# A two-problem attention decode on one core: softmax weights placed between the V matmuls of the last group, V sums by scaled adds, query projection with half the matmuls

## The chip, the cores and the metric

The kernel runs on one core of a Trainium2 chip. The metric is the device time in microseconds; the kernel before takes 250.23 us as the median of 7 runs (249.08 to 252.08). The engines named below are PE (TensorE, matmuls; PEld is its weight load), DVE (VectorE), ACT (ScalarE), POOL (GpSimd) and SP (SyncE, which here issues nearly all DMAs).

## The reference

Two problems, A and B, with the same shapes: one token `x` (576 wide), 32 query heads over 16 key/value heads, head size 128, 8192 cached positions. A attends to the last W = 2048 positions, B to all 8192. Everything is bf16.

```python
# the same for A (last W positions of the caches) and for B (all of them)
q = (x @ wq).reshape(B, Sq, Hq, Dh).transpose(0, 2, 1, 3)
k = jnp.repeat(k_cache, rep, axis=1)        # rep = 2 query heads to a kv head
v = jnp.repeat(v_cache, rep, axis=1)
scores = jnp.einsum("bhqd,bhkd->bhqk", q, k) * (Dh ** -0.5)
p = softmax(scores, axis=-1)
o = jnp.einsum("bhqk,bhkd->bhqd", p, v)
out = o.transpose(0, 2, 1, 3).reshape(B, Sq, Hq * Dh) @ wo
...
return jnp.concatenate([a, b], axis=-1)
```

## The kernel before

**Data.** About 102.8 MB are read once: `wq` of A and B (4.6 MB each), the K and V caches that are used (five groups of about 16.8 MB) and `wo` of A and B. Group 0 holds all 16 kv heads of A, groups 1 to 4 hold four kv heads of B each (`NG = 5`). A group's K and V lie in four SBUF slots, two for K and two for V; a slot is loaded anew when PE has read it for the last time in the group before. `wq` and `wo` use the same slots ahead of the first and after the last group.

**Stages of a group** (`for g in range(NG)`, L658 to L679). `q_stage` puts the group's query columns into `qst`. `k_transpose` (L460) turns K with PE in eight units; ACT (L472) and DVE (L475) copy the result from PSUM to `kt`. `k_scores` (L480, matmuls L487) adds the scores of all units up in one PSUM bank. `softmax_exp` (L499) takes the maximum, then exp on ACT. `softmax_transpose` (L513) turns the probabilities and DVE writes them, masked, to `ptm` (L527). `v_slot` (L532, matmuls L540) multiplies them with V, 32 matmuls of 512 columns per slot; `opsum` then holds for each row eight blocks of 128 columns, of which the row needs those that belong to its head. `v_keep` (L545) masks all eight blocks into `diag` (L548) and sums them by a reduce (L384, the line of the helper `sums`) into `acc`.

**Query projection** (L411 to L444). The contraction of 576 is cut in nine steps of 64 rows of `wq`; a row's columns are split over a pair of partitions. `x_columns` writes columns of `x`, masked by the parity of the partition, to `xpad`; `q_part` (L417, matmuls L425) runs 9 x 2 x 4 matmuls of 512 columns, into two banks; `q_finish` copies the banks to `qrow` (ACT L431, DVE L433) and turns them with eight small matmuls (L438) into `qcol`. It is done for A, then for B. `wq` of B lies where K slot 1 and the first part of V slot 0 of group 0 go.

**The end.** In the last group, between `softmax_transpose` and `v_slot`, `weights` (L555) works out from the maxima and sums of all rows a factor for each row: three pairs of small fp32 matmuls, `turn` (L558), `back` (L576), `total` (L588), with short DVE and ACT steps between them. `combine(0)` (L602) scales A's `acc` (L599) and adds A's partial rows up per head with fp32 matmuls (L612), also ahead of the last group's V. After the loop `combine(1)` does that for groups 1 to 4. Then `wo_part` (L622, matmuls L627) runs 128 matmuls of 144 columns for A and 128 for B, `finish_out` (L632) copies each result (L633) and SP sends it (L639). `wo` of A is one load, `wo` of B four (L681 to L690): 24 rows into K slot 1, then 5, 2 and 1 rows into V slot 0 and behind, the first of these three after the last group's reads of V slot 0.

**Order of work.** `add` (L53) records operations in program order; each engine runs its own in that order, and waits come from what each operation reads and writes. DVE, ACT, POOL and SP are unrolled. PE runs its part of the groups as a loop of five passes (L231) with one body: an operation's `loop=(g, place, cond)` gives its place in the body, and neighbouring places with the condition `LAST` (the last group only) are put together in an `If` (L227), a branch on PE.

Of the kernel before, what the change touches and what calls it, by code (L numbers as in the profile page):

```python
# [275 lines left out]
def bass_concat_heads__sliding_block_cached__gqa_block_cached__decode_kernel(  # L276
# [37 lines left out]
    sameB = nc.alloc_sbuf_tensor("sameB", [128, 128], F32)  # L314
    selq = nc.alloc_sbuf_tensor("selq", [128, 4], BF16)
    onesf = nc.alloc_sbuf_tensor("onesf", [128, 4], F32)
    qst = nc.alloc_sbuf_tensor("qst", [128, 2 * 264], BF16)
    qcol = nc.alloc_sbuf_tensor("qcol", [128, 2, HQ], BF16)
    xtwo = nc.alloc_sbuf_tensor("xtwo", [128, 2, 8], BF16)
    xpad = nc.alloc_sbuf_tensor("xpad", [128, 2, 10, 32], BF16)  # L320
    par2 = nc.alloc_sbuf_tensor("par2", [128, 2], F32)
    maskV = nc.alloc_sbuf_tensor("maskV", [128, 8], F32)
    qrow = nc.alloc_sbuf_tensor("qrow", [128, 1024], BF16)
    stat = nc.alloc_sbuf_tensor("stat", [128, 40], F32)
    srow = nc.alloc_sbuf_tensor("srow", [4, 2, 160], F32)
    diag = nc.alloc_sbuf_tensor("diag", [128, 8, DH], F32)
    acc = nc.alloc_sbuf_tensor("acc", [128, NG, DH], F32)
# [43 lines left out]
    def select(t, base_, pattern, mult):  # L371
        return lambda pool: pool.affine_select(out=t, in_=t, compare_op=ALU.not_equal, fill=1.0,
                                               base=base_, pattern=pattern, channel_multiplier=mult)

    add("pool", select(ident[:], 0, [[-1, 128]], 1), reads=["ident"], writes=["ident"])
    add("pool", select(selq[:], 0, [[-32, 4]], 1), reads=["selq"], writes=["selq"])
    for dj in range(-3, 4):
# [31 lines left out]


    def x_columns(P):  # L411
        for e in range(2):
            add("dve", lambda dve, e=e: dve.tensor_scalar(xpad[:, P, 5 * e:5 * e + 5, 0], xtwo[:, P, 0:5],  # L413
                                                          par2[:, e:e + 1], None, ALU.mult),
                reads=[("xtwo", P), "par2"], writes=[("xpad", P)])

    def q_part(P, off, res):  # L417
        def mm(pe):
            for u in range(9):
                for c in range(2):  # L420
                    for j in range(4):
                        n_ = 2 * j + c
                        x = u // 2 if n_ // 4 == u % 2 else 5 + (u + 1) // 2
                        o = off + u * 2048 + (n_ % 4) * 512
                        ins = pe.matmul(opsum[32 * j:32 * j + 32, c * 512:(c + 1) * 512], lhsT=xpad[:, P, x, :],  # L425
                                        rhs=slots[:, o:o + 512], start=(u == 0), stop=(u == 8))
            return ins
        add("pe", mm, reads=[("xpad", P)] + res, writes=B_O)

    def q_finish(P):  # L430
        add("act", lambda act: act.activation(qrow[:, 0:512], opsum[:, 0:512], ACT.Copy),  # L431
            reads=[B_O[0]], writes=[("qrow", 0)])
        add("dve", lambda dve: dve.tensor_copy(qrow[:, 512:1024], opsum[:, 512:1024]),  # L433
            reads=[B_O[1]], writes=[("qrow", 1)])

        def tr(pe):
            for i in range(8):
                ins = pe.matmul(misc[:, i * 4:(i + 1) * 4], lhsT=qrow[:, i * 128:(i + 1) * 128],  # L438
                                rhs=selq[:, :], start=True, stop=True)
            return ins  # L440
        add("pe", tr, reads=[("qrow", 0), ("qrow", 1), "selq"], writes=[B_M])
        add("dve", lambda dve: dve.tensor_copy(qcol[:, P, :].rearrange("p (j i) -> p i j", j=4),
                                               misc[:, 0:32].rearrange("p (i j) -> p i j", j=4)),
            reads=[B_M], writes=[("qcol", P)])  # L444
# [51 lines left out]
    def st(col, n=1):  # L496
        return stat[:, col:col + n]
# [33 lines left out]

    def v_slot(g, s, place):  # L532
        v = slots[:, voff(s):voff(s) + SLOT].rearrange("p (m y) -> p m y", m=4)

        def mm(pe):
            for tt in range(8):
                for j in range(4):
                    o = tt * 128 + 32 * j
                    b = (8 * j + tt) * 128
                    ins = pe.matmul(opsum[32 * j:32 * j + 32, s * 512:(s + 1) * 512], lhsT=ptm[:, o:o + 32],  # L540
                                    rhs=v[:, :, b:b + 128], start=(tt == 0), stop=(tt == 7), skip_group_check=True)
            return ins
        add("pe", mm, reads=["ptm"] + VS[s], writes=[B_O[s]], loop=(g, place, None))

    def v_keep(g):  # L545
        def go(dve):
            m = bass.AP(tensor=maskV, offset=0, ap=[[8, 128], [1, 8], [0, DH]])
            return dve.tensor_tensor(diag[:, :, :], opsum[:, :].rearrange("p (y d) -> p y d", y=8), m, ALU.mult)  # L548
        add("dve", go, reads=B_O + ["maskV"], writes=["diag"], tag="keep")
        sums(acc[:, g, :], diag[:, :, :].rearrange("p y d -> p d y"), ["diag"], [("acc", g)])  # L550


    LAST = lambda g: g == NG - 1

    def weights(g):  # L555
        at = [(g, 18.1 + k / 8, LAST) for k in range(3)]

        def turn(pe):  # L558
            pe.matmul(misc[0:1, 0:128], lhsT=st(C_M), rhs=identf[:, :], start=True, stop=True)  # L559
            return pe.matmul(misc[0:4, 128:256], lhsT=st(C_M + 1, 4), rhs=identf[:, :], start=True, stop=True)  # L560
        add("pe", turn, reads=[("st", C_M + c) for c in range(NG)] + ["identf"], writes=[B_M], loop=at[0])

# [11 lines left out]
        add("dve", rep, reads=["srow"], writes=["srow2"])  # L574

        def back(pe):  # L576
            pe.matmul(misc[:, 256:257], lhsT=srow[0:1, 0, 32:160], rhs=onesf[0:1, 0:1], start=True, stop=True)  # L577
            return pe.matmul(misc[:, 257:261], lhsT=srow[0:4, 1, 32:160], rhs=identf[0:4, 0:4], start=True, stop=True)  # L578
        add("pe", back, reads=["srow2", "ones", "identf"], writes=[B_M], loop=at[1])
        add("dve", lambda dve: dve.scalar_tensor_tensor(st(C_T, NG), st(C_M, NG), SCALE, misc[:, 256:261],  # L580
# [5 lines left out]
            reads=[("st", C_W)] + [("st", C_L + c) for c in range(NG)], writes=[("st", C_T + 5)])  # L586

        def total(pe):  # L588
            pe.matmul(misc[:, 264:265], lhsT=same[:, :], rhs=st(C_T + 5), start=True, stop=True)  # L589
            return pe.matmul(misc[:, 265:269], lhsT=sameB[:, :], rhs=st(C_T + 6, 4), start=True, stop=True)  # L590
        add("pe", total, reads=[("st", C_T + 5), "same", "sameB"], writes=[B_M], loop=at[2])
        add("dve", lambda dve: dve.reciprocal(st(C_T + 10, NG), misc[:, 264:269]),
# [4 lines left out]

    def scaled(g):
        add("dve", lambda dve: dve.tensor_scalar(accs[:, g, :], acc[:, g, :], st(C_AL + g), None, ALU.mult),  # L599
            reads=[("acc", g), ("st", C_AL)], writes=[("accs", g)])  # L600

    def combine(P, loop=None):  # L602
        groups = range(1, NG) if P else [0]
        for g in groups:
            scaled(g)

        def mm(pe):
            for g in groups:
                for r in range(4):
                    w = pickB[:, r, :] if P else pick[:, r, :]  # L610
                    to = misc[32 * (g - 1):32 * g, 0:32] if P else misc[:, 0:32]
                    ins = pe.matmul(to, lhsT=w, rhs=accs[:, g, 32 * r:32 * r + 32], start=(r == 0), stop=(r == 3))  # L612
            return ins
        add("pe", mm, reads=["pickB" if P else "pick"] + [("accs", g) for g in groups], writes=[B_M], loop=loop)
        add("dve", lambda dve: dve.tensor_copy(opj[:, P, 0:32], misc[:, 0:32]), reads=[B_M], writes=[("opj", P)])

# [41 lines left out]
    for g in range(NG):  # L658
        for s in range(2):
            load_kv(ks, g, s, koff(s), KS[s], "k")  # L660
        for s in range(2):
            load_kv(vs, g, s, voff(s), VS[s], "v")
        for s in range(2):
            q_stage(g, s)
        k_transpose(g, 0, 0)
        k_transpose(g, 1, 1)
        for u in range(2, 8):
            k_scores(g, u - 2, 2 * u)
            k_transpose(g, u, 2 * u + 1)
        k_scores(g, 6, 16)  # L670
        k_scores(g, 7, 17)
        softmax_exp(g)
        softmax_transpose(g, 18)
        if g == NG - 1:
            weights(g)
            combine(0, (g, 18.6, LAST))
        v_slot(g, 0, 20)
        v_slot(g, 1, 21)
        v_keep(g)  # L679

# [6 lines left out]
    for k, (P, lo, n, off, res) in enumerate(wo_loads):  # L687
        if res[0][0] == "w":
            wo_loads[k] = (P, lo, n, off, res)
        load_wo(P, lo, n, off, res)  # L690
    combine(1)
    for P in range(2):
# [35 lines left out]
```

## Time and profile before

The profile is one execution with the hardware profiler. "Busy" is the time in which an engine worked; the line numbers are those of the listing.

| what | value |
|---|---|
| time of 7 runs | median 250.23 us, 249.08 to 252.08 |
| profiled execution, device time | 251.18 us |
| its span, first to last instruction | 249.7 us |
| mean granted TensorE clock | 0.835 of full |
| DMA, mean rate over the span | 412 GB/s, 102.89 MB |
| PE / PEld busy | 165.2 us / 117.3 us |
| DVE / ACT busy | 87.3 us / 87.3 us |
| q matmuls L425 | x144, 11.5 us |
| V matmuls L540 | x320, 28.4 us |
| mask L548 and reduce L384 of the V sums | x5 each, 1225 ns and 1871 ns |
| combine L612 | x8 with `pick` 1.9 us, x32 with `pickB` 1.4 us |
| projection matmuls L627 | x256, 6.4 us |

A group is read as: line, engine, operation, how many, busy time or mean of one. An fp32 matmul appears as two records, so the 4 and 16 matmuls of the two combines stand as x8 and x32. Matmuls overlap their weight loads, so the busy times of PE and PEld are not added.

### The profile page before, as it was taken

What the parts mean: (1) busy time and instruction counts of PE and PEld (TensorE: products, weight loads), DVE (VectorE), ACT (ScalarE), POOL (GpSimd) and SP (SyncE); (2) the same over time, 40 slices, a digit from 0 to 9 for tenths busy, and PEclk for the clock granted to TensorE, in tenths of its full rate; (3) what the DMA queues carried; (4) which work ended last, traced back from release to release, by engine and by line L of the source; (5) the groups of instructions that cost most, each with busy time, mean ns of one, the idle gap of its engine ahead of it and who ended that gap; (6) DMA issues with size and microseconds to landing.
All of it is one profiled execution on the core that took longest, in us unless ns stands there. A gap on an engine that the chain in (4) does not pass through costs nothing. (4 is left out here: it accounts for less than half of the span.)

```text
span 249.7 us, 5439 instructions
## 1 busy us (share of the span) xinstructions
PE 165.2 (66%) x2428; PEld 117.3 (47%) x2428; DVE 87.3 (35%) x140; ACT 87.3 (35%) x95; POOL 10.7 (4%) x48
## 2 busy tenths in 40 slices
PE   0027739993725999463999471999570899558474
PEld 0003329781315876223886221987330878345163
DVE  0001034553141555231656222456314355431500
ACT  2000017873002786101778100677500578500000
POOL 7400000000000000000000000000000000000000
PEclk9999797999595999775999775699978699955759
DMA  9998999999999999999999999999999999999970
GB/s 337 419 431 373 424 392 417 424 424 419 450 430 436 430 446 432 420 430 430 426 430 446 436 425 430 430 425 430 446 425 436 425 436 425 430 437 433 428 307 7
DMA packets 5929, 102.89 MB, mean 412 GB/s; under 512 B 928, under 2 KB 1056, under 8 KB 1312
## 3 DMA queue, kind: packets, MB, share of 16 engines
q1 hardware_dynamic: 5632, 102.77, 96.8%
q8 instruction: 6, 0.10, 0.2%
q10 hardware_dynamic: 288, 0.00, 0.1%
q14 instruction: 3, 0.02, 0.0%
HBM read 102.76 MB, written 0.00 MB: 412 GB/s over the span
## 5 line engine op out<-in xcount | busy, mean ns | idle before, releaser
L472 ACT ACTIVATE kt<-ktps 128x1024 bf16<-128x1024 bf16 x80 | 78.4, 1021 | 89.1 <-PE ktps L466 89.1
L466 PE MATMUL ktps<-ident,slots 128*128 128x128 bf16 x1280 | 87.5, 233 | 33.2 <-PEq L214 30.9
L466 PEld LDWEIGHTS ktps<-ident,slots 128*128 128x128 bf16 x1280 | 81.3, 105 | 48.7 <-issue 48.5
L475 DVE COPY kt<-ktps 128x1024 bf16<-128x1024 bf16 x80 | 55.3, 692 | 69.5 <-PE ktps L466 69.5
L540 PE MATMUL opsum<-slots,ptm 128*32 128x512 bf16 x320 | 28.4, 533 | 4.2 <-PEq L214 4.2
L487 PE MATMUL sacc<-kt,qst 128*32 128x512 bf16 x320 | 25.4, 393 | 1.8 <-PEq L214 1.8
L425 PE MATMUL opsum<-slots,xpad 128*32 128x512 bf16 x144 | 11.5, 490 | 19.8 <-DVE xpad L413 19.8
L540 PEld LDWEIGHTS opsum<-slots,ptm 128*32 128x32 bf16 x320 | 11.6, 128 | 19.6 <-issue 17.2
L425 PEld LDWEIGHTS opsum<-slots,xpad 128*32 128x32 bf16 x144 | 5.1, 119 | 25.2 <-issue 23.6
L548 DVE TENSOR_TENSOR diag<-opsum,maskV 128x1024 f32<-128x1024 f32 x5 | 6.1, 1225 | 29.0 <-PE opsum L540 29.0
L518 PE MATMUL misc<-ident,psb 128*128 128x128 bf16 x40 | 4.1, 264 | 11.5 <-PEq L214 11.5
L431 ACT ACTIVATE qrow<-opsum 128x512 bf16<-128x512 f32 x2 | 1.2, 597 | 28.3 <-PE opsum L425 28.3
L456 POOL COPY qst<-qcol 128x8 bf16<-128x8 bf16 x20 | 3.1, 191 | 165.5 <-PE sacc L487 150.6
L508 ACT ACTIVATE psb<-sacc,stat 128x1024 bf16<-128x1024 f32 x5 | 5.6, 1113 | 11.8 <-DVE stat L502 11.8
L518 PEld LDWEIGHTS misc<-ident,psb 128*128 128x128 bf16 x40 | 3.1, 117 | 14.0 <-issue 14.0
L384 DVE TENSOR_REDUCE acc<-diag 128x128 f32<-128x1024 f32 x5 | 9.4, 1871 | 0.2
L487 PEld LDWEIGHTS sacc<-kt,qst 128*32 128x32 bf16 x320 | 5.0, 94 | 7.9 <-issue 4.2
L527 DVE TENSOR_SCALAR ptm<-misc,par 128x512 bf16<-128x512 bf16 x10 | 4.4, 480 | 11.2 <-PE misc L518 11.2
L627 PE MATMUL ktps<-slots,opj 128*32 128x144 bf16 x256 | 6.4, 268 | 2.7 <-issue 2.7
L627 PEld LDWEIGHTS ktps<-slots,opj 128*32 128x32 bf16 x256 | 5.7, 118 | 3.2 <-issue 3.2
L413 DVE TENSOR_SCALAR xpad<-xtwo,par 128x5 bf16<-128x5 bf16 x4 | 0.7, 232 | 14.5 <-DMA xtwo<-in_A_x_dram 13.0
L433 DVE CAST qrow<-opsum 128x512 bf16<-128x512 f32 x2 | 1.4, 692 | 11.8 <-PE opsum L425 11.8
(60 smaller groups left out, 35.3 us busy)
## 6 DMA issues: line engine op xcount, KB each, us to landing
slots<-in_B_k_cache_dram SPq DMA_DIRECT2D x8, 4096.0 KB
slots<-in_B_v_cache_dram SPq DMA_DIRECT2D x8, 4096.0 KB
slots<-in_A_k_cache_dram SPq DMA_DIRECT2D x8, 1024.0 KB
slots<-in_A_v_cache_dram SPq DMA_DIRECT2D x8, 1024.0 KB
slots<-in_A_wq_dram SPq DMA_DIRECT2D x1, 4608.0 KB, 13.9
slots<-in_B_wq_dram SPq DMA_DIRECT2D x1, 4608.0 KB, 24.7
slots<-in_A_wo_dram SPq DMA_DIRECT2D x1, 4608.0 KB, 19.5
slots<-in_B_wo_dram SPq DMA_DIRECT2D x1, 3456.0 KB, 27.4
```

What stands on the lines that cost most here:

```text
L384: add("dve", lambda dve: dve.tensor_reduce(out, view, AX.X, ALU.add), reads=reads, writes=writes, tag=tag)
L425: ins = pe.matmul(opsum[32 * j:32 * j + 32, c * 512:(c + 1) * 512], lhsT=xpad[:, P, x, :], rhs=slots[:, o:o + 512], start=(u == 0), stop=( ...
L466: ins = pe.matmul(ktps_bf[q][:, t * 128:(t + 1) * 128], lhsT=slots[:, o:o + 128], rhs=ident[:, :], start=True, stop=True, is_transpose=True)
L472: add("act", lambda act, q=q, dst=dst: act.activation(dst, ktps_bf[q], ACT.Copy), reads=[("bank", q)], writes=[("kt", u % NKT, q)], tag="e ...
L475: add("dve", lambda dve, q=q, dst=dst: dve.tensor_copy(dst, ktps_bf[q]), reads=[("bank", q)], writes=[("kt", u % NKT, q)], tag="e%d%d" % ( ...
L487: ins = pe.matmul(sacc[32 * j:32 * j + 32, :], lhsT=qst[:, o:o + 32], rhs=rhs, start=(u == 0 and e == 0), stop=True, skip_group_check=True)
L508: return act.activation(psb[:, :].rearrange("p (x g) -> p x g", g=2), src, ACT.Exp, bias=st(C_NB + g), scale=SCALE, accum_out=st(C_L + g))
L518: ins = pe.matmul(dst[:, t * 128:(t + 1) * 128], lhsT=psb[:, t * 128:(t + 1) * 128], rhs=ident[:, :], start=True, stop=True, is_transpose= ...
L527: ins = dve.tensor_scalar(to, src, par2[:, e:e + 1], None, ALU.mult)
L540: ins = pe.matmul(opsum[32 * j:32 * j + 32, s * 512:(s + 1) * 512], lhsT=ptm[:, o:o + 32], rhs=v[:, :, b:b + 128], start=(tt == 0), stop=( ...
L548: return dve.tensor_tensor(diag[:, :, :], opsum[:, :].rearrange("p (y d) -> p y d", y=8), m, ALU.mult)
L627: ins = pe.matmul(ktps[P][32 * j:32 * j + 32, 0:OUTW], lhsT=opj[:, P, jj:jj + 32], rhs=slots[:, o:o + OUTW], start=(jj == 0), stop=(jj == ...
```

## The change

The query projection now uses 36 matmuls for each problem: `xpad` carries two columns per step, one for each half of the output columns, and `q_part` writes both halves at once into one bank; `q_finish` has one copy and four turning matmuls. `v_keep` is called once for each slot and adds four blocks with a factor from a mask column, directly from PSUM; in the last group the factor is `wlast`, the mask times the last group's softmax factor, and the sum goes straight to `accs`. `v_slot` is cut in halves of 16 matmuls. `weights` is cut in three parts, which stand in the last group ahead of the first V half, between the halves of slot 0, and after slot 0. `combine` of groups 0 to 3 stands between the halves of slot 1, ahead of the last V matmuls; after the loop only group 4 is combined. A's result column copy (`o_columns(0)`) stands before the last half. PE's conditional pieces in the loop body are now four instead of one.

```diff
-    selq = nc.alloc_sbuf_tensor("selq", [128, 4], BF16)
+    selq = nc.alloc_sbuf_tensor("selq", [128, 4, 2], BF16)
-    xpad = nc.alloc_sbuf_tensor("xpad", [128, 2, 10, 32], BF16)
+    xpad = nc.alloc_sbuf_tensor("xpad", [128, 2, 9, 32], BF16)
-    qrow = nc.alloc_sbuf_tensor("qrow", [128, 1024], BF16)
+    qrow = nc.alloc_sbuf_tensor("qrow", [128, 512], BF16)
-    diag = nc.alloc_sbuf_tensor("diag", [128, 8, DH], F32)
+    wlast = nc.alloc_sbuf_tensor("wlast", [128, 8], F32)
...
-    add("pool", select(selq[:], 0, [[-32, 4]], 1), reads=["selq"], writes=["selq"])
+    add("pool", select(selq[:], 0, [[-32, 4], [-1, 2]], 1), reads=["selq"], writes=["selq"])
...
     def x_columns(P):
-        for e in range(2):
-            add("dve", lambda dve, e=e: dve.tensor_scalar(xpad[:, P, 5 * e:5 * e + 5, 0], xtwo[:, P, 0:5],
-                                                          par2[:, e:e + 1], None, ALU.mult),
+        for u, n, col, i, e in ((0, 5, 0, 0, 0), (0, 5, 1, 0, 1), (1, 4, 0, 1, 1), (1, 4, 1, 0, 0)):
+            dst = bass.AP(tensor=xpad, offset=(P * 9 + u) * 32 + col, ap=[[576, 128], [64, n]])
+            add("dve", lambda dve, dst=dst, i=i, n=n, e=e: dve.tensor_scalar(dst, xtwo[:, P, i:i + n], par2[:, e:e + 1],
+                                                                             None, ALU.mult),
                 reads=[("xtwo", P), "par2"], writes=[("xpad", P)])
     def q_part(P, off, res):
         def mm(pe):
             for u in range(9):
-                for c in range(2):
-                    for j in range(4):
-                        n_ = 2 * j + c
-                        x = u // 2 if n_ // 4 == u % 2 else 5 + (u + 1) // 2
-                        o = off + u * 2048 + (n_ % 4) * 512
-                        ins = pe.matmul(opsum[32 * j:32 * j + 32, c * 512:(c + 1) * 512], lhsT=xpad[:, P, x, :],
-                                        rhs=slots[:, o:o + 512], start=(u == 0), stop=(u == 8))
-            return ins
-        add("pe", mm, reads=[("xpad", P)] + res, writes=B_O)
+                for j in range(4):
+                    o = off + u * 2048 + j * 512
+                    ins = pe.matmul(opsum[32 * j:32 * j + 32, P * 512:(P + 1) * 512], lhsT=xpad[:, P, u, :],
+                                    rhs=slots[:, o:o + 512], start=(u == 0), stop=(u == 8))
+            return ins
+        add("pe", mm, reads=[("xpad", P)] + res, writes=[B_O[P]])
     def q_finish(P):
-        add("act", lambda act: act.activation(qrow[:, 0:512], opsum[:, 0:512], ACT.Copy),
-            reads=[B_O[0]], writes=[("qrow", 0)])
-        add("dve", lambda dve: dve.tensor_copy(qrow[:, 512:1024], opsum[:, 512:1024]),
-            reads=[B_O[1]], writes=[("qrow", 1)])
+        add("act", lambda act: act.activation(qrow[:, :], opsum[:, P * 512:(P + 1) * 512], ACT.Copy),
+            reads=[B_O[P]], writes=["qrow"])
         def tr(pe):
-            for i in range(8):
-                ins = pe.matmul(misc[:, i * 4:(i + 1) * 4], lhsT=qrow[:, i * 128:(i + 1) * 128],
-                                rhs=selq[:, :], start=True, stop=True)
-            return ins
-        add("pe", tr, reads=[("qrow", 0), ("qrow", 1), "selq"], writes=[B_M])
-        add("dve", lambda dve: dve.tensor_copy(qcol[:, P, :].rearrange("p (j i) -> p i j", j=4),
-                                               misc[:, 0:32].rearrange("p (i j) -> p i j", j=4)),
+            for i in range(4):
+                ins = pe.matmul(misc[:, i * 8:(i + 1) * 8], lhsT=qrow[:, i * 128:(i + 1) * 128],
+                                rhs=selq[:, :, :].rearrange("p j h -> p (j h)"), start=True, stop=True)
+            return ins
+        add("pe", tr, reads=["qrow", "selq"], writes=[B_M])
+        add("dve", lambda dve: dve.tensor_copy(qcol[:, P, :].rearrange("p (h j i) -> p i j h", h=2, j=4),
+                                               misc[:, 0:32].rearrange("p (i j h) -> p i j h", i=4, j=4)),
             reads=[B_M], writes=[("qcol", P)])
...
         add("dve", put, reads=[B_M, "par2"], writes=["ptm"], tag="put")
-    def v_slot(g, s, place):
+    def v_slot(g, s, half, place):
         v = slots[:, voff(s):voff(s) + SLOT].rearrange("p (m y) -> p m y", m=4)
         def mm(pe):
-            for tt in range(8):
+            for tt in range(4 * half, 4 * half + 4):
                 for j in range(4):
                     o = tt * 128 + 32 * j
                     b = (8 * j + tt) * 128
...
             return ins
         add("pe", mm, reads=["ptm"] + VS[s], writes=[B_O[s]], loop=(g, place, None))
-    def v_keep(g):
-        def go(dve):
-            m = bass.AP(tensor=maskV, offset=0, ap=[[8, 128], [1, 8], [0, DH]])
-            return dve.tensor_tensor(diag[:, :, :], opsum[:, :].rearrange("p (y d) -> p y d", y=8), m, ALU.mult)
-        add("dve", go, reads=B_O + ["maskV"], writes=["diag"], tag="keep")
-        sums(acc[:, g, :], diag[:, :, :].rearrange("p y d -> p d y"), ["diag"], [("acc", g)])
+    def v_keep(g, s):
+        last = g == NG - 1
+        dst = accs[:, g, :] if last else acc[:, g, :]
+        res = ("accs" if last else "acc", g)
+        for m in range(4):
+            w = (wlast if last else maskV)[:, 4 * s + m:4 * s + m + 1]
+            src = opsum[:, s * 512 + m * 128:s * 512 + (m + 1) * 128]
+            if s == 0 and m == 0:
+                add("dve", lambda dve, w=w, src=src: dve.tensor_scalar(dst, src, w, None, ALU.mult),
+                    reads=[B_O[s], "wlast" if last else "maskV"], writes=[res], tag="keep")
+            else:
+                add("dve", lambda dve, w=w, src=src: dve.scalar_tensor_tensor(dst, src, w, dst, ALU.mult, ALU.add),
+                    reads=[B_O[s], "wlast" if last else "maskV", res], writes=[res], tag="keep")
     LAST = lambda g: g == NG - 1
-    def weights(g):
-        at = [(g, 18.1 + k / 8, LAST) for k in range(3)]
-
+    def weights_top(g):
         def turn(pe):
             pe.matmul(misc[0:1, 0:128], lhsT=st(C_M), rhs=identf[:, :], start=True, stop=True)
             return pe.matmul(misc[0:4, 128:256], lhsT=st(C_M + 1, 4), rhs=identf[:, :], start=True, stop=True)
-        add("pe", turn, reads=[("st", C_M + c) for c in range(NG)] + ["identf"], writes=[B_M], loop=at[0])
+        add("pe", turn, reads=[("st", C_M + c) for c in range(NG)] + ["identf"], writes=[B_M], loop=(g, 18.5, LAST))
         def top(dve):
             dve.tensor_reduce(srow[0:1, 0, 0:32], misc[0:1, 0:128].rearrange("p (j h) -> p h j", j=4), AX.X, ALU.max)
...
             return dve.tensor_scalar(srow[0:4, 1, 32:160].rearrange("p (a r) -> p a r", r=8), src, -SCALE, None, ALU.mult)
         add("dve", rep, reads=["srow"], writes=["srow2"])
+    def weights_exp(g):
         def back(pe):
             pe.matmul(misc[:, 256:257], lhsT=srow[0:1, 0, 32:160], rhs=onesf[0:1, 0:1], start=True, stop=True)
             return pe.matmul(misc[:, 257:261], lhsT=srow[0:4, 1, 32:160], rhs=identf[0:4, 0:4], start=True, stop=True)
-        add("pe", back, reads=["srow2", "ones", "identf"], writes=[B_M], loop=at[1])
+        add("pe", back, reads=["srow2", "ones", "identf"], writes=[B_M], loop=(g, 20.1, LAST))
         add("dve", lambda dve: dve.scalar_tensor_tensor(st(C_T, NG), st(C_M, NG), SCALE, misc[:, 256:261],
                                                         ALU.mult, ALU.add),
             reads=[B_M] + [("st", C_M + c) for c in range(NG)], writes=[("st", C_T)])
...
         add("dve", lambda dve: dve.tensor_tensor(st(C_T + 5, NG), st(C_W, NG), st(C_L, NG), ALU.mult),
             reads=[("st", C_W)] + [("st", C_L + c) for c in range(NG)], writes=[("st", C_T + 5)])
+    def weights_sum(g):
         def total(pe):
             pe.matmul(misc[:, 264:265], lhsT=same[:, :], rhs=st(C_T + 5), start=True, stop=True)
             return pe.matmul(misc[:, 265:269], lhsT=sameB[:, :], rhs=st(C_T + 6, 4), start=True, stop=True)
-        add("pe", total, reads=[("st", C_T + 5), "same", "sameB"], writes=[B_M], loop=at[2])
+        add("pe", total, reads=[("st", C_T + 5), "same", "sameB"], writes=[B_M], loop=(g, 20.3, LAST))
         add("dve", lambda dve: dve.reciprocal(st(C_T + 10, NG), misc[:, 264:269]),
             reads=[B_M], writes=[("st", C_T + 10)])
         add("dve", lambda dve: dve.scalar_tensor_tensor(st(C_AL, NG), st(C_W, NG), 2.0, st(C_T + 10, NG),
                                                         ALU.mult, ALU.mult),
             reads=[("st", C_T + 10), ("st", C_W)], writes=[("st", C_AL)])
-    def scaled(g):
-        add("dve", lambda dve: dve.tensor_scalar(accs[:, g, :], acc[:, g, :], st(C_AL + g), None, ALU.mult),
-            reads=[("acc", g), ("st", C_AL)], writes=[("accs", g)])
-
-    def combine(P, loop=None):
-        groups = range(1, NG) if P else [0]
-        for g in groups:
-            scaled(g)
-
+        add("dve", lambda dve: dve.tensor_scalar(wlast[:, :], maskV[:, :], st(C_AL + NG - 1), None, ALU.mult),
+            reads=["maskV", ("st", C_AL)], writes=["wlast"])
+        for k in range(NG - 1):
+            add("dve", lambda dve, k=k: dve.tensor_scalar(accs[:, k, :], acc[:, k, :], st(C_AL + k), None, ALU.mult),
+                reads=[("acc", k), ("st", C_AL)], writes=[("accs", k)])
+    def combine(groups, loop=None):
         def mm(pe):
             for g in groups:
                 for r in range(4):
-                    w = pickB[:, r, :] if P else pick[:, r, :]
-                    to = misc[32 * (g - 1):32 * g, 0:32] if P else misc[:, 0:32]
+                    w = pickB[:, r, :] if g else pick[:, r, :]
+                    to = misc[32 * (g - 1):32 * g, 304:336] if g else misc[:, 272:304]
                     ins = pe.matmul(to, lhsT=w, rhs=accs[:, g, 32 * r:32 * r + 32], start=(r == 0), stop=(r == 3))
             return ins
-        add("pe", mm, reads=["pickB" if P else "pick"] + [("accs", g) for g in groups], writes=[B_M], loop=loop)
-        add("dve", lambda dve: dve.tensor_copy(opj[:, P, 0:32], misc[:, 0:32]), reads=[B_M], writes=[("opj", P)])
+        add("pe", mm, reads=["pick", "pickB"] + [("accs", g) for g in groups], writes=[B_M], loop=loop)
+    def o_columns(P):
+        add("dve", lambda dve: dve.tensor_copy(opj[:, P, 0:32], misc[:, 272 + 32 * P:304 + 32 * P]),
+            reads=[B_M], writes=[("opj", P)])
     def load_wo(P, lo, n, off, res):
...
         softmax_exp(g)
         softmax_transpose(g, 18)
         if g == NG - 1:
-            weights(g)
-            combine(0, (g, 18.6, LAST))
-        v_slot(g, 0, 20)
-        v_slot(g, 1, 21)
-        v_keep(g)
+            weights_top(g)
+        v_slot(g, 0, 0, 20)
+        if g == NG - 1:
+            weights_exp(g)
+        v_slot(g, 0, 1, 20.2)
+        if g == NG - 1:
+            weights_sum(g)
+        v_keep(g, 0)
+        v_slot(g, 1, 0, 21)
+        if g == NG - 1:
+            combine(range(NG - 1), (g, 21.2, LAST))
+            o_columns(0)
+        v_slot(g, 1, 1, 21.5)
+        v_keep(g, 1)
     wo_loads = [
         (0, 0, 32, 0, [("k", 0), ("k", 1, 0)]),
...
         load_wo(P, lo, n, off, res)
-    combine(1)
+    combine([NG - 1])
+    o_columns(1)
     for P in range(2):
         for Q, lo, n, off, res in wo_loads:
             if Q == P:
```

## Prediction, made before the changed kernel ran

> **What bounds the kernel now.** I read the page's slices first, then transfers by line, then the chain of waits from its end backward.
>
> ```profile
> PEclk9999797999595999775999775699978699955759
> DMA  9998999999999999999999999999999999999970
> q8 instruction: 6, 0.10, 0.2%
> slots<-in_B_wo_dram SPq DMA_DIRECT2D x1, 3456.0 KB, 27.4
> slots<-in_B_wo_dram SPq DMA_DIRECT2D x1, 720.0 KB, 12.8
> slots<-in_B_wo_dram SPq DMA_DIRECT2D x1, 288.0 KB, 13.1
> slots<-in_B_wo_dram SPq DMA_DIRECT2D x1, 144.0 KB, 13.0
> ```
>
> Each digit of the DMA row covers 6.24 us: the 16 DMA engines are full from 1.3 us to about 241. Nothing that makes an engine faster before 241 shortens the run, unless the DMA queue had run dry there, and it doesn't (in-flight packets average 15.3 of 16 at worst, around 35 us). The last number of the B_wo lines is the time from issue to landing. With the issue times of the timeline (215.06, then 231.37, 231.74, 232.21) they land at 242.4, 244.1, 244.8 and 245.2. So what can be won lies in the last 8 us:
>
> ```profile
> 227.79 5.89 PE opsum L540 x63
> 233.68 0.02 issue
> 233.70 1.24 DVE diag L548
> 234.94 0.02 issue
> 234.96 1.87 DVE acc L384
> 236.83 0.79 DVE accs L599 x4
> 237.62 0.04 issue
> 237.67 1.20 PE misc L612 x29
> 238.87 3.40 PE ktps L627 x92
> 242.27 1.35 issue
> 243.62 2.18 PE ktps L627 x127
> 245.80 1.38 issue
> 247.18 0.55 PE ktps L627 x21
> 247.73 0.02 issue
> 247.75 0.31 DVE outsb L633
> ```
>
> Columns: start, length, what. The last V (L540), sums (L548, L384), scaling (L599), head combine (L612), output projections of A and then B (L627). The landings bind nothing here: B's matmuls begin at about 244.2 (20 of the 127 still belong to A, whose result is copied at 244.17), 1.8 us after 242.4, and its last 21 come at 247.18, 2 us after 245.2. The two "issue" gaps, 2.73 us together, are PE waiting for its own code: of the six 16 KB packets of q8, four fall before 67 us and two at 241.3 and 244.8, just ahead of the gaps; 127 matmuls with as many weight loads between the gaps are 254 instructions, one block (an estimate: 256 of 64 bytes).
>
> From PE's last matmul to the span's end it is 2.0 us (249.73 - 247.73: copy 0.31, issue and landing of a 1 KB output).
>
> **The change, part by part.**
>
> *q from half the matmuls.* L425 falls from 72 to 36 matmuls per problem and L438 from 8 to 4; two tiny xpad writes are added (L413 rows: 0.23 us each). At 5.76 us for 72, q of B ends 2.9 us earlier, less 0.3. This lies under the DMA row; k loads of group 0 issue earlier and fill a dip of under 0.1 us. Worth 0 to -0.1 us. DVE's qrow copy goes (0.69), ACT's stays; hidden too. Its real effect is on code: 72+72+8+8 = 160 PE instructions fewer ahead of the loop.
>
> *V sums.* Per group, L548 1.22 + L384 1.87 = 3.1 us become eight scaled adds of 128x128 from PSUM. No row shows such an add. The nearest is L599, the same size from SBUF: 0.28 each, 0.20 stepping back to back. An eighth of L548 (0.15) is the lower bound; with every add waiting for its predecessor I bound it above by 0.4. I take 0.25: four after the last V matmul make 1.0 us (0.6 to 1.6). Groups 0 to 3: PE waits 6.1 to 7.3 us for K there anyway; 0.
>
> *Weights between V matmuls.* New PE order from ptm ready (220.39): turn 1.03 (L559+L560) to 221.4; V half 1.48 (a quarter of 5.93) to 222.9, over DVE's 0.9 us for L564 to L573; back 1.02 to 223.9; V half to 225.4, over stat and exp (0.17+0.21+0.18 and handovers); total 1.02 to 226.4; V half to 227.9. DVE from 226.4: reciprocal, weight, wlast, four accs: 0.20+0.18+0.15+0.80 and handovers, 227.9 to 228.1. Combine of groups 0 to 3: 1.91 (pick) + 24/32 of 1.20 = 2.8 to 230.9. Last half to 232.4, adds 1.0 to 233.4, combine of group 4 0.3 + handovers: A's projection starts at **233.8 instead of 238.8**. Three more branches round the conditional pieces: the one in a non-last group takes 0.37 us on PE's sequencer, so up to 1.1 us per group, inside the 6 us wait; in the last group the end moves to 234.9 at worst.
>
> *What is late next.* A's projection: 128 matmuls at 33.7 ns (108 in 238.63 to 242.27) = 4.3, so 238.1. B's then waits for its 3456 KB at 242.4, 4.3 us later. Hence all of V, sums and combine has 4.3 us of cover, and their errors above cost nothing. The three small B_wo loads wait for V slot 0: issued at 225.4 instead of 231.4. SP has nothing else queued behind them but the outputs, yet the engines have A_wo and B_wo ahead of them until 241, so they land as before (0; bounds -0.5 to +0.5).
>
> B's 128 matmuls from 242.4 then set the end, and their price is the clock. Rows: 33.7 ns at granted 0.5, 17.2 ns (127 in 2.18) at 1.0.
>
> ```profile
> 232.40:235.80 3.40, 1.25 (x24) 0.41 (x16) 2.06 (x2) 0.00 (x0) 0.00 (x0) 1.00 1.00 431
> 235.80:239.20 3.40, 1.53 (x51) 1.53 (x55) 1.95 (x6) 0.00 (x0) 0.00 (x0) 0.50 0.90 384
> 242.60:246.00 3.40, 2.18 (x127) 2.00 (x128) 0.31 (x1) 0.00 (x0) 0.00 (x0) 0.99 0.12 42
> ```
>
> Stretches with PE busy first and the granted clock third from the end: after a stretch with PE busy 1.25 of 3.4 us, the next ran at 0.5; B ran at 0.99 because A kept PE busy just before. The rule that speaks against the change is in the Trainium skill, "TensorE: Matmul & The Clock Gate", What's actually happening: an idle window of about 3.4 us puts the clock at half, and a busy one is needed to get it back. The new 4.3 us hole before B is such an idle window. By the clock of the old B the matmuls take 2.2 us, but the last landing (245.2 + 4 matmuls) gives 245.35, end 247.35, **-2.4**. By the rule they take 4.3 us: 242.43 + 4.31 = 246.75, end 248.75, **-1.0**. The 1.25-of-3.4 row is nearest to the new hole, so I take -1.0.
>
> *Code.* 160 instructions less, a few more for branches and waits: boundaries move later in the projections by some 77 matmuls. The one after A's 108th comes at B's 57th, the next at 235+77 = 312, beyond 256: one late block vanishes. The one before, one block further back (old: in the combine after the loop), comes at A's 57th; in the old run the code behind it was there in time, having been fetched in the loop's first pass. The block for B's 57th can be asked for from A's 57th on, at 235.7, and is needed at 244.3. In the old kernel 243.62 to 247.18, 3.6 us, passed between entering one block and having the next; under full DMA, by the packets, 5 to 10. I take it as there in time: 0, bound +1.5 (asked for only at 242.4: there at 246.0, 71 matmuls at 33.7 ns to 248.4, end 250.4).
>
> **Sum** against the profiled run's own 249.73: 248.75, -0.98. That run was 251.18 in all (1.45 outside the span), 0.95 above the median; I take its excess for something both kernels have, so 250.23 - 1.0 = **249.2**.
>
> **Rivals.**
>
> 1. *Landings alone set the end.* B runs at the full clock, or the lagging engine that brings the last B_wo rows is earlier: 247.85 from the sum above, down to 247. For it: windows are not aligned to the program, and busy shares of 64% (2.18 of 3.4) kept the clock. Against it: 4.3 us of nothing.
>
> 2. *The code wait stays on the path*, as bounded: end 250.4, +0.7, 250.9. For it: four fetches under full DMA were slow, and one stalled PE in the first pass. Against it: over 8 us of notice.
>
> 3. *Slower: the loop no longer stays in PE's instruction memory.* Old boundaries count back from the 108th matmul in steps of one block: the loop lay in four blocks, its start a little (some 135 instructions) behind a boundary. With 160 fewer ahead of it the start falls before that boundary: five blocks, six with the one prefetched.
>
> ```profile
> 58.89 0.38 PE L466 MATMUL ktps<-ident,slots 128*128 128x128 bf16 x4 [2.23 <-issue]
> ```
>
> That is a block arriving late in the first pass (timeline; the bracket is the wait): 2.23 us. The Trainium skill, "Runtime: NRT & Kernel Launch", Instruction fetch mechanics, gives PE 128 KiB (eight blocks of 16 KiB) but also says that only a two-page window is kept and a taken branch out of it costs a fetch. By the two-page rule the old loop would have refetched on every pass; between 70 and 240 us there is no q8 packet, so at least five blocks stayed. If five are all, every pass fetches all: 5 x 2.23 = 11.2 us less 6.9 of slack = 4.3, times 4 passes = +17, about 267. It decides from the sixth block on. Eight blocks by the page against five proved: unlikely.
>
> 4. *The change doesn't shorten the chain* (V, combine and weights stall each other by more than 4.3 us): 250 to 252. The sum has no wait of that size.
>
> **How the numbers follow.** Forecast 50%, rival 1 20%, rival 2 14%, rival 3 7%, rival 4 and others 9%. The forecast's own range is 248.2 to 250.2 (landing ±0.5, run-to-run ±0.5). A measurement tells some 0.5% from no change, 248.98 to 251.48. Faster: all of rival 1 and about half of the forecast, 0.45. Same: the other half, rival 2, some of rival 4: 0.38. Slower: rival 3 and the rest, 0.17. The range 247.2 to 251.0 leaves out the loop's reload and the extremes.
>
> **What would show it.** A's projection starts near 234 and B's after a hole that ends at 242.4 by a DMA, not by "issue"; granted clock 0.5 over B; B's length 4.3 us; one L627 issue gap or none; q8 packets five or six, none between 75 and 230 us. Wrong if: q8 packets recur in every pass (rival 3); B at 17 ns (rival 1); A starts after 238 (rival 4); the B_wo landings move by over 1 us.

## The result, and the profile after

The changed kernel takes **248.47 us** (median of 14 runs, 247.9 to 249.5) against 250.23 (35 runs of the kernel before): ratio 0.9932, 95% interval 0.9915 to 0.9950. That is 1.8 us less. The forecast was 249.2 with a range of 247.2 to 251.0.

The profiled execution has a span of 246.9 us. Its chain of waits from 236 us on (start, length, what), its transfers by line (last number: us from issue to landing), and, ahead of them, its row of q8, the queue whose 16 KB packets the prediction reads as PE's code:

```profile
213.55 27.69 DMA slots<-in_B_wo_dram
241.24 0.04 issue
241.28 3.59 PE ktps L634 x128
244.88 0.02 issue
244.90 0.31 DVE outsb L640
```

```profile
q8 instruction: 6, 0.10, 0.2%
...
slots<-in_B_wo_dram SPq DMA_DIRECT2D x1, 3456.0 KB, 27.7
slots<-in_B_wo_dram SPq DMA_DIRECT2D x1, 720.0 KB, 18.4
slots<-in_B_wo_dram SPq DMA_DIRECT2D x1, 288.0 KB, 18.8
slots<-in_B_wo_dram SPq DMA_DIRECT2D x1, 144.0 KB, 18.6
```

Where the old chain went back through V, mask, reduce and combine and had two "issue" waits of 1.35 and 1.38 us inside the projections, the new one has a transfer: B's 24 rows of `wo`, landed at 241.24. B's 128 matmuls follow in one piece, then the copy. The three small loads are issued at 224.5 to 225.4 instead of 231.4 to 232.2 and take 5.6 us more from issue to landing: they land 1.2 us earlier, as the 24 rows do, so the earlier issue itself brought nothing that can be seen. PE's work ahead of B and in B, over the last windows (the columns are PE busy with its count, then PEld, DVE, ACT, POOL, granted clock, DMA share, GB/s):

```profile
237.40:240.80 3.40, 0.37 (x18) 0.18 (x6) 0.31 (x1) 0.00 (x0) 0.00 (x0) 1.00 0.86 351
240.80:244.20 3.40, 2.92 (x100) 2.92 (x104) 0.00 (x0) 0.00 (x0) 0.00 (x0) 0.50 0.42 161
244.20:246.90 2.70, 0.64 (x40) 0.45 (x28) 0.31 (x1) 0.00 (x0) 0.00 (x0) 1.00 0.00 0
```

PE worked 0.37 of 3.4 us ahead of B, and B ran at half the clock until 244.2, when it came back.

### The profile page after: what moved, and what is told of

It is laid out like the page before. It is cut to its first block, busy times and chain, and to the rows that moved or that the text cites. A ratio compares the mean times of both kernels' runs of the same rounds, so it can differ in the third digit from the quotient of the medians.

```text
span 246.9 us, 5330 instructions
## 1 busy us (share of the span) xinstructions
PE 166.6 (67%) x2348; PEld 117.9 (48%) x2348; DVE 84.8 (34%) x172; ACT 87.2 (35%) x95; POOL 10.7 (4%) x48
## 5 line engine op out<-in xcount | busy, mean ns | idle before, releaser
L538 PE MATMUL opsum<-slots,ptm 128*32 128x512 bf16 x320 | 33.1, 579 | 5.8 <-PEq L214 5.8
L538 PEld LDWEIGHTS opsum<-slots,ptm 128*32 128x32 bf16 x320 | 12.8, 132 | 21.0 <-issue 19.4
L425 PE MATMUL opsum<-slots,xpad 128*32 128x512 bf16 x72 | 8.1, 629 | 21.7 <-DVE xpad L416 21.7
L425 PEld LDWEIGHTS opsum<-slots,xpad 128*32 128x32 bf16 x72 | 2.9, 140 | 25.1 <-issue 25.1
L555 DVE SCALAR_TENSOR_TENSOR acc<-opsum,maskV,acc 128x128 f32<-128x128 f32 x28 | 9.8, 351 | 7.3 <-PE opsum L538 6.4
L634 PE MATMUL ktps<-slots,opj 128*32 128x144 bf16 x256 | 7.6, 310 | 3.5 <-DMA slots<-in_B_wo_dram 3.5
L634 PEld LDWEIGHTS ktps<-slots,opj 128*32 128x32 bf16 x256 | 7.2, 141 | 3.7 <-DMA slots<-in_B_wo_dram 3.7
L416 DVE TENSOR_SCALAR xpad<-xtwo,par 128x5 bf16<-128x5 bf16 (+1 forms) x8 | 1.3, 232 | 16.0 <-DMA xtwo<-in_A_x_dram 12.9
L552 DVE TENSOR_SCALAR acc<-opsum,maskV 128x128 f32<-128x128 f32 x4 | 1.4, 351 | 15.0 <-PE opsum L538 15.0
L498 DVE TENSOR_REDUCE stat<-sacc 128x1 f32<-128x512 f32 x5 | 3.5, 692 | 4.4 <-PE sacc L485 4.4
```

The lines of the kernel that those rows point to most:

```text
L425: ins = pe.matmul(opsum[32 * j:32 * j + 32, P * 512:(P + 1) * 512], lhsT=xpad[:, P, u, :], rhs=slots[:, o:o + 512], start=(u == 0), stop=( ...
L498: add("dve", lambda dve: dve.tensor_reduce(st(C_M + g), sacc[:, :], AX.X, ALU.max), reads=[B_S], writes=[("st", C_M + g)], tag="max")
L555: add("dve", lambda dve, w=w, src=src: dve.scalar_tensor_tensor(dst, src, w, dst, ALU.mult, ALU.add), reads=[B_O[s], "wlast" if last else ...
L634: ins = pe.matmul(ktps[P][32 * j:32 * j + 32, 0:OUTW], lhsT=opj[:, P, jj:jj + 32], rhs=slots[:, o:o + OUTW], start=(jj == 0), stop=(jj == ...
```

## The experiments

The theory after the result: the end was a PE chain with two late code blocks in it, and is now "B's rows landed + 128 matmuls + 2.0 us". Whatever takes some 2 us off the PE chain should reach this new limit, so the parts of the change should not add up. The rivals: the V chain (weights, sums) makes the gain; or the code position makes it; or the lag of one DMA engine in the old profile is a property of the kernels.

Each median is of 6 to 12 runs. They came from two chips, at three times; the ratio is always to the kernel before, run beside them.

| kernel | median us | before beside it | ratio, 95% interval |
|---|---|---|---|
| q_alone | 248.26 | 250.3 | 0.9928, 0.9904 to 0.9951 |
| v_alone | 248.50 | 250.3 | 0.9945, 0.9914 to 0.9977 |
| code_only | 248.41 | 250.3 | 0.9928, 0.9903 to 0.9954 |
| split_wo | 248.03 | 250.3 | 0.9918, 0.9885 to 0.9950 |
| weights_front | 248.71 | 249.75 | 0.9958, 0.9939 to 0.9977 |
| sums_old | 248.28 | 249.75 | 0.9940, 0.9919 to 0.9962 |
| both_old | 247.94 | 249.75 | 0.9926, 0.9898 to 0.9954 |
| code_full | 249.85 | 250.2 | 0.9998, 0.9969 to 1.0027 |
| warm8 | 247.90 | 250.2 | 0.9899, 0.9869 to 0.9930 |
| split_warm | 247.80 | 250.2 | 0.9893, 0.9862 to 0.9924 |
| after_again | 248.68 | 250.2 | 0.9936, 0.9902 to 0.9969 |

### The kernel before, a second profile

> The kernel before once more, for a second profile. If the DMA engine that landed B's rows 1.5 us after the other fifteen belonged to that one execution, the lag is under 0.5 us here and the 24 rows land at about 241; the two waits for code in the projections stay, 1.3 to 1.4 us each. If the lag belongs to the kernel, it is 1.5 us again.

No edit; one execution, 249.27 us, span 247.8. Its chain of waits at the end:

```profile
237.10 3.40 PE ktps L627 x105
240.50 1.22 issue
241.72 2.18 PE ktps L627 x127
243.90 1.38 issue
245.28 0.55 PE ktps L627 x21
245.83 0.02 issue
245.85 0.31 DVE outsb L633
```

The two waits are there again, at the same matmuls. The 24 rows landed at 240.45 by the semaphore updates of the 16 DMA engines, the slowest of them 0.10 us after the fifteenth; in the first profile it was 1.53 us (242.41 against 240.88). In none of the ten other profiles that load the 24 rows at once is it over 0.5 us. So the lag belonged to that execution, while the two code waits came in both.

### The query projection alone, and V alone

```diff
# q_alone: the kernel before with the new selq, xpad, qrow, x_columns, q_part, q_finish
-                        ins = pe.matmul(opsum[32 * j:32 * j + 32, c * 512:(c + 1) * 512], lhsT=xpad[:, P, x, :],
+                    ins = pe.matmul(opsum[32 * j:32 * j + 32, P * 512:(P + 1) * 512], lhsT=xpad[:, P, u, :],
...
# v_alone: the changed kernel with the old selq, xpad, qrow, x_columns, q_part, q_finish
```

> The kernel before with only the new query projection (160 PE instructions fewer ahead of the loop). Code-position theory: no wait for code in A's projection, at most one short one near B's 57th matmul, A still starts at about 238.8; the tail loses 1.4 us and up to 2.4 where the landings allow it: 248.9 us (248.0 to 249.4). Rival, the V chain (sums and weights) made the whole gain: 250.2, within 0.3 of the kernel before.

> The changed kernel with the old query projection (code longer by 160 instructions again). Cover theory: A's projection starts at about 234, a wait for code near A's 105th matmul disappears in the hole before B's data, none is seen in B: 248.5 to 249.0, like the full change. Rival, the code position made the gain: 250.2.

Each half gives what the whole gives: 0.9928 and 0.9945 against 0.9932. q_alone's chain, with the V part as it was:

```profile
214.31 26.53 DMA slots<-in_B_wo_dram
240.84 0.04 issue
240.88 1.12 PE ktps L623 x60
242.00 1.14 issue
243.15 1.28 PE ktps L623 x68
```

A ran without a code wait; B waited for its data until 240.84 and then for code after its 60th matmul (expected at the 57th). So q_alone does not end where the changed kernel does for the same reason. From the landing of the 24 rows to B's last matmul it took 3.58 us, at the full clock but with 1.14 us of waiting for code; the changed kernel took 3.63 us, with no such wait but mostly at the half clock. The two prices happen to be alike. v_alone's projections of A (its last part) and B:

```profile
234.64 2.16 PE L638 MATMUL ktps<-slots,opj 128*32 128x144 bf16 x122
241.85 4.03 PE L638 MATMUL ktps<-slots,opj 128*32 128x144 bf16 x128 [5.05 <-DMA slots<-in_B_wo_dram]
```

There is neither a code wait in B nor the one that was expected near A's 105th matmul: that block was there in time; PE idled 5.05 us before B. The rival that gives the whole gain to the V chain falls with q_alone, the one that gives it to the code position alone falls with v_alone.

### Useless code: 48 and 128 matmuls more

```diff
+    def idle_code(pe):
+        for k in range(48):        # code_only; range(128) in code_full
+            ins = pe.matmul(ktps[0][:, 0:4], lhsT=ident[:, :], rhs=selq[:, :], start=True, stop=True)
+        return ins
+    add("pe", idle_code, reads=["ident", "selq"], writes=[("bank", 0)])
     sums(maskV[:, :], same...
```

> The kernel before with 48 useless small matmuls (96 PE instructions) after the query projection, so that code blocks end where they do after 160 instructions less; nothing else changes. Code-position theory: one wait for code instead of two, 1.4 us less in spite of more work: 248.9 (248.3 to 249.4). Rival, code position does not matter: 250.2 to 250.4.

> Control for code_only: the kernel before with 128 useless small matmuls (256 PE instructions, one whole code block) after the query projection. Code blocks end where they do in the kernel before. Code-position theory: two waits for code again, after A's 108th matmul and B's 107th, 250.0 to 250.4 (no change against before). Rival, the useless matmuls themselves help (by their time, or by keeping PE busy): 248.4, as with 48.

The kernel before with 48 matmuls more is 0.7% faster; with 128 more it is as before. Both have more to do at the start, and code_full shows that this costs nothing that can be seen; between the two it matters where the blocks end. The chain of code_only, then of code_full:

```profile
240.93 1.12 PE ktps L627 x59
242.05 0.39 issue
242.44 1.22 PE ktps L627 x65
243.66 0.04 issue
243.70 0.28 PE ktps L627 x4
```

```profile
235.52 2.96 PE ktps L627 x103
238.48 2.42 issue
240.90 2.18 PE ktps L627 x127
243.08 1.38 issue
244.46 0.55 PE ktps L627 x21
```

In code_only B begins when its data land (240.89) and waits 0.39 us for code; in code_full the two waits are back at the old matmuls, 3.8 us together. I had expected 1.4 us for code_only and got 1.9 (250.30 - 248.41) by medians: the wait in A is gone, and the one in B is shorter. The two profiled executions lie 1.0 and 1.4 us below their kernels' medians (247.43, 248.46), so these chains show where the waits are; how long they usually are is not shown.

### The V parts undone in the changed kernel

```diff
# weights_front: all three parts of the weights at PE places 18.5, 18.6, 18.7, ahead of V;
# their calls in the program move ahead of V too
-        ... loop=(g, 20.1, LAST)    and    loop=(g, 20.3, LAST)
+        ... loop=(g, 18.6, LAST)    and    loop=(g, 18.7, LAST)
# sums_old: one mask over all eight blocks, then a reduce, after the last V matmul
-        v_keep(g, 0)
...
+            return dve.tensor_tensor(diag[:, :, :], opsum[:, :].rearrange("p (y d) -> p y d", y=8), m, ALU.mult)
+        sums(dst, diag[:, :, :].rearrange("p y d -> p d y"), ["diag"], [("accs" if last else "acc", g)])
# both_old: the two together
```

> The changed kernel with all three parts of the weights ahead of V again (combine of groups 0 to 3 stays before the last V half). V and A's projection come 1.6 us later (0.95 + 0.69 us in which PE waits for DVE). Cover theory: inside the 3.5 us hole before B, so no change: 248.5 (248.2 to 248.8). Rival, the interleaving is a gain by itself: 249.5 to 250.1.

> The changed kernel with the old V sums (mask of all eight blocks, then reduce: 3.1 us instead of 1.5 us after the last V matmul). Cover theory: A's projection 1.6 us later, hidden in the hole: 248.5 (248.2 to 248.8). Rival, the sums are a gain by themselves: 249.5 to 250.1.

> Weights ahead of V and the old sums together in the changed kernel: A's projection 3.2 us later, which is about the whole hole of 3.5 us. Cover theory: 248.4 to 249.0, B perhaps at the full clock since no idle window is left. Rival, the chain of V carries the gain: 250.2, as before the change.

No single one and not both together bring the old time back; the three intervals all hold the changed kernel's 0.9932 or lie within 0.1% of it, and weights_front alone may cost a little (0.9958). The chain of both_old:

```profile
213.91 27.50 DMA slots<-in_B_wo_dram
241.42 0.04 issue
241.46 3.85 PE ktps L632 x128
```

A transfer again, and PE idled 3.08 us before it. A's projection began at 234.5, only 0.6 us later than in the changed kernel's profile, not 3.2: V's last 16 matmuls ran at the full clock here (13 of them took 1.03 us instead of 1.89). So both_old did not use up the cover, and B's clock was not full as I had thought possible (3.85 us). Where the cover ends was not tried.

Two of these profiles, and that of after_again (the changed kernel once more, below), show a second cover that neither the prediction nor this theory had: A's projection waited for A's own weights. It did so for 0.41 us in weights_front, for 1.02 in sums_old, and in after_again:

```profile
229.66 0.44 PE L616 MATMUL misc<-accs,pickB 128*32 128x32 f32 x8 [1.68 <-DVE accs L555]
232.67 3.46 PE L634 MATMUL ktps<-slots,opj 128*32 128x144 bf16 x128 [2.58 <-DMA slots<-in_A_wo_dram]
```

Where the V chain is that early, making it earlier still does not even start A earlier.

### B's clock and B's landing

```diff
# split_wo
-        (1, 0, 24, WQ_W, [("k", 1, 1)]),
+        (1, 0, 12, WQ_W, [("k", 1, 1)]),
+        (1, 12, 12, WQ_W + 12 * DM, [("w", 2)]),
# warm8: after finish_out(0), 8 of these; split_warm: split_wo and 7 of them after B's first 12 rows
+                    ins = pe.matmul(ktps[2][:, :], lhsT=ident[:, :], rhs=kt[:, 0, 0:512], start=True, stop=True)
```

> The changed kernel with B's 3456 KB output weights as two loads of 12 rows instead of one of 24. Theory, B's 128 matmuls after one landing set the end: 48 of them start some 2 to 4 us earlier, the end falls to the last landing + 2.1 us: 247.7 to 248.0 (0.5 to 0.8 under the changed kernel). Rival, the last small load sets the end already: 248.4 to 248.6.

> The changed kernel with 8 useless matmuls of 512 columns (1.7 us at the full clock, 3.4 at half) in the hole between A's and B's projection. Clock theory: B's 128 matmuls run at 17 ns (2.2 us instead of 3.5 to 4.3), the last landing sets the end: 0.5 to 0.8 us under the changed kernel run beside it, 247.7 to 248.0. Rival, the last landing sets the end already, or the clock ignores them: no change.

> split_wo (B's 24 rows as two loads) with 7 such useless matmuls after B's first 12 rows. Both tools: last landing + 2.1 us, 247.4 to 247.8, the least of all. If split_wo already sits on the last landing: 248.0, as without them.

> The changed kernel beside the three on the same chip, for comparison: 248.3 to 248.6, B's 24 rows landed at 240.5 to 241.3, one hole before B, no wait for code in the projections.

The PE rows of warm8 from its eight extra matmuls on (the bracket is the idle time before and what ended it), then two windows, with the columns as above:

```profile
237.07 1.90 PE L717 MATMUL ktps<-kt,ident 128*128 128x512 bf16 x8
240.87 2.22 PE L634 MATMUL ktps<-slots,opj 128*32 128x144 bf16 x116 [1.90 <-DMA slots<-in_B_wo_dram]
243.28 0.61 PE L634 MATMUL ktps<-slots,opj 128*32 128x144 bf16 x12 [0.20 <-DMA slots<-in_B_wo_dram]
```

```profile
236.70:240.10 3.40, 2.27 (x30) 0.95 (x21) 0.31 (x1) 0.00 (x0) 0.00 (x0) 1.00 0.88 366
240.10:243.50 3.40, 2.40 (x124) 1.93 (x124) 0.00 (x0) 0.00 (x0) 0.00 (x0) 1.00 0.55 211
```

With PE busy 2.27 of 3.4 us in the stretch that holds most of the hole, the clock stays at 1.00, 116 of B's matmuls take 2.22 us, and PE waits for the small loads. after_again, beside it on the same chip, took 4.06 us for its 128 after a landing at 240.87, and has no wait for code in the projections that the extra matmuls could have shifted away. warm8 is 0.78 us under after_again by medians, split_warm 0.88 (6, 6 and 7 runs; the three ratios' intervals to the kernel before overlap, but only two runs of warm8 and one of split_warm are slower than the fastest of after_again). split_wo, measured at another time, is 0.14% below the changed kernel's ratio, inside both intervals, so its own share isn't shown. warm8 and split_warm are the versions shown to be below the changed kernel too; with them the last landing (243.60 and 243.72) sets the end.

## Why the prediction was right, and what it mis-sized

- **The DMA row as the wall, the last 8 us as the field:** held. The loads stayed where they were in the queue: issued 6.8 us earlier, the small ones landed 1.2 us earlier, as the 24 rows before them did.
- **The new PE order:** A's projection was to start at 233.8 and started at 233.88. That it met the number so closely was luck. Terms inside the sum were off and cancelled: a V half occupied PE for 1.8 to 2.1 us instead of 1.48, the scaled adds cost 0.35 each and 1.51 for four (I took 1.0, bound 1.6), and the last group's `ptm` was ready at 219.0, 1.4 us earlier in the span than in the first profile. The last need not be the change: in the second profile of the kernel before it was ready at 218.3. The sum also left out A's own weights, which in the profile it was read from landed only at 234.2 (issued at 214.68, 19.5 us to landing), after the start it forecast; here they landed at 233.0.
- **The cover behind it:** predicted 4.3 us, seen 3.52 (4.78 in after_again). Its consequence, that the V parts' errors cost nothing, is borne out by weights_front, sums_old and both_old.
- **B at half clock:** right in kind, 0.5 until 244.2; 3.56 us instead of 4.31 here, because the clock came back with 40 matmuls to go, and 4.03 in after_again. warm8 shows that these microseconds were the clock's.
- **Code:** one late block vanishes, the other is hidden: no "issue" wait in the projections, the last two q8 packets at 238.92 (in the hole) and 243.04, none between 75 and 230 us. Rival 3 (the loop falling out of PE's memory) did not happen, though by the prediction's count the loop now lies over five blocks.
- **What failed in size was the landing term.** The step "they land as before (0; bounds -0.5 to +0.5)", said of the small loads, and the 242.4 for the 24 rows were taken from one profile in which one DMA engine was 1.5 us behind; here the 24 rows landed at 241.24, in after_again at 240.87, and in the second profile of the kernel before at 240.45. They moved by 1.2 us, more than the 1 us that the prediction had named as a sign of being wrong. The old chain did not feel that lag, since it came later anyway; the new one ends on it. By spans the account is -0.98 predicted, -1.17 for the landing, -0.72 for B's clock: -2.87 against a measured -2.85. By medians the change is -1.8 us, since the profiled execution of the kernel before lay 0.95 above its own median; I had taken that excess for something both kernels have, and the changed kernel's profiled execution lies 0.1 above its median (248.56, 248.47). So the two terms that came out better than forecast, 1.9 us together, were in good part balanced by this one, and that the forecast lies within 0.8 us of the result is partly luck.
- **What the sum did not say:** it booked the gain on the V chain and priced the code at 0 beside it. q_alone, v_alone and code_only show that either alone brings B's last matmul to 3.1 to 4.1 us after the landing; the changed V work adds nothing measurable on top of the shorter code, and the reverse. With the code alone B keeps the full clock and pays part of a code wait; with the V chain alone it pays the half clock.

## What to carry to other kernels

Before pricing the parts of a change to the tail, find the next limit (here the landing of the last weights): parts that each reach it do not add up, and here 96 instructions of padding, which compute nothing, gained as much as the whole change. Where an engine streams short instructions after a loop, look for "issue" gaps a constant number of instructions apart (here 254) with a q8 packet ahead of each: here that was code arriving late, and moving the block ends is an edit of its own. And read a limit that has been hidden so far from more than one execution, because the kernel's time has not yet tested the one value that a profile gives.

## What the runs showed of the hardware that was not expected

- A late code block cost between 0.39 us (code_only) and 2.42 us (code_full). In all eight such waits in the projections (two each in both profiles of the kernel before and in code_full, one each in q_alone and code_only) PE went on 2.3 to 2.5 us after the q8 packet began and 1.2 to 1.5 us after it ended. What differs is when the packet began: 2.03 us before PE ran out of code in code_only, 0.11 us in code_full. What sets that moment was not tried.
- q_alone, v_alone and code_only show one q8 packet in the middle of the loop's passes (at 147.8, 188.7 and 147.8 us); the kernels before and after show none between 75 and 230 us. It cost nothing visible. Why it comes so late stays open, and so does whether it brought v_alone the block that was expected late in A.
- A's 1 KB output, issued at 238.14 in the changed kernel while the DMA queue was full, landed at 244.05; B's, issued at 245.24 into an empty queue, at 246.83.
- V's 64 matmuls of the last group ran at half or full clock in different executions of the same code: 16 of them took 1.90 us in the changed kernel's first profile and 1.05 us in its second, after_again.
